# Weight-conversion passes regrouped at the end of a step's VectorE work, in an attention + rational-MLP kernel

## The chip, the cores and the metric

The kernel runs on one core of a Trainium2 chip. The time is device microseconds of that core, the median of repeated runs.

## What is computed

Attention over 4 batches and 8 heads (576 positions, head size 64) with a position bias, then an MLP whose nonlinearity is a quotient of two polynomials:

```python
    scores = scale * np.matmul(q, k.transpose(0, 1, 3, 2))
    scores = scores + bias.transpose(2, 0, 1)[None, :, :, :]
    attn = softmax(scores)
    x = (attn @ v) as (2304, 512)
    h = x @ w_in                                # 512 -> 2048
    P = a[0] + a[1] * h + a[2] * h**2 + a[3] * h**3
    Q = 1.0 + np.abs(b[0]) * np.abs(h) + np.abs(b[1]) * h**2
    out = (P / (Q + 1e-06)) @ w_out             # 2048 -> 512
```

`w_in` and `w_out` come as 64-bit floats and are turned into a high and a low 32-bit part on the chip.

## The kernel before

**Two halves.** Attention fills the first 270 us. The MLP fills the rest. Its 2304 rows are cut into five blocks (384, 512, 512, 512, 384 rows, `TS`, L27), and its 2048 hidden features into 16 groups of 128. Two passes over the five blocks are made, each with half of the features, because the split weights of one half fill the buffers. A block takes four **steps** (`FPR` = 4) of 256 features each, so there are 40 steps, counted from 0: steps 0 to 3 are block 0 of pass one, 4 to 7 block 1, 16 to 19 block 4, and 20 to 39 pass two.

**A step s** (the loop at L853) issues, in this order: the first product `mm1(s)` on TensorE (24 matmuls, `h` in PSUM, from the split rows `xh`, `xl` and the split weights); the second product `mm2(s-2)` (output tiles `o`); for step s-1, three ScalarE operations `rat1` (L725 to L727, the reciprocal of Q by Ln and Exp), three VectorE operations `dv2`, `dv3`, `dv4` (L746, L753, L760: `gh`, the high part of the quotient, and `m`); `evac` (L813: ScalarE copies finished output tiles of a block out of PSUM); for step s, `rat0` (L720, L721: two ScalarE reads of `h`), and `dvu`, `dv0`, `dv1` (L730, L736, L739: three VectorE operations that read `h` from PSUM); for step s-1 `pl1` (L767: GpSimd makes `gl`, the low part of the quotient, from `m`). Then, in even steps, `split_x` (L302, L303) splits half of the rows of the next block, and SyncE loads the rows of the block after it. All queues keep the order in which the program writes (`tc.manual_schedule()`).

**The late weights.** Ten of the 16 feature groups are converted during attention. Those of the last six (`LATE`) are converted inside pass one: 12 **jobs**, one for each group and matrix. A job (`w_conv`, L116) is a load of the same 0.5 MB twice at two offsets (`wx`, `wy`, L126), and five passes over 128x512 words: `mag` (L142, VectorE), `rebias` (L151, ScalarE), and on VectorE `sign` (L154), `join` (L167) and `low` (L174); then two stores of the result to DRAM (L114), which pass two loads again (`w_load`, L231). The buffers of `wx` and `wy` are one pool of three tiles.

Before, the jobs are placed in half steps, one job every three halves (L833 to L850): half 2s comes ahead of `rat0(s)`, half 2s+1 at the end of step s. The first job has its `mag` in half 2, the next in half 5, and so on; `sign`, `join` and `low` follow two halves after `mag`, and right behind them the load of the next job is issued, one half step ahead of that job's own `mag`. So every second job has `sign`, `join`, `low` right behind `dv4`, and `mag` at the end of a step; the others have it the other way round.

**Across blocks.** `mm2` of a new block writes the PSUM tiles of the block before, so it waits for `evac`. `evac` stands behind `rat1(s-1)` in ScalarE's queue, and `rat1(s-1)` waits for `dvu(s-1)` on VectorE. `e_norm(NU - 1)` (L400, one VectorE product and a store) finishes the last attention tile inside step 4; rows of it are read by the load at the end of step 6.

Of the kernel before, what the change touches and what calls it, by code (L numbers as in the profile page):

```python
# [8 lines left out]
F32 = mybir.dt.float32  # L9
# [7 lines left out]
P = 128  # L17
# [18 lines left out]
def tile_attn_moe(  # L36
# [14 lines left out]
    cpool = ctx.enter_context(tc.tile_pool(name="cpool", bufs=1))  # L51
# [31 lines left out]
        for d_, nm in ((woh, "woh"), (wol, "wol")):  # L83
            d_[g] = pool.tile([P, 2, DM], F32R, tag=f"{nm}{g}", name=f"{nm}{g}")

    fill = cpool.tile([P, 112], F32, tag="fill", name="fill")
    nc.gpsimd.memset(fill[:, 0:8], 0.0)
    stg = ctx.enter_context(tc.tile_pool(name="stg", bufs=2))
    bpool = ctx.enter_context(tc.tile_pool(name="bpool", bufs=2))
# [4 lines left out]
    U16 = mybir.dt.uint16  # L94
    FN = KD * P
# [13 lines left out]
    def w_out_to(f, part, hi, lo):  # L109
        d = wsc.get((f, part)) or dpool.tile([P, 2, KD, P], F32, tag=f"ws{f}_{part}", name=f"ws{f}_{part}")  # L110
        wsc[f, part] = d
        for i, t in enumerate((hi, lo)):
            if t is not None:
                nc.sync.dma_start(out=d[:, i], in_=t.bitcast(F32))  # L114

    def w_conv(f, part):  # L116
        st = {}
        here = f < 6
        eng = G if f < KF - LATE else V

        def load():
            w = (w_in, w_out)[part]

            def get(nm, o, src):
                t = stg.tile([P, 4 * FN + 4], U16, tag="wx", name=f"{nm}{f}_{part}", bufs=3)
                nc.sync.dma_start(out=t[:, o:o + 4 * FN], in_=src)  # L126
                return t

            x = get("wx", 0, w.bitcast(U16)[f])[:, 0:4 * FN]
            st["u"] = x.bitcast(U32).rearrange("p (f t) -> p f t", t=2)[:, :, 1]  # L130
            if eng is G:
                st["h"] = x.rearrange("p (f t) -> p f t", t=4)[:, :, 1:3]
            else:
                y = get("wy", 1, w.bitcast(U16)[f])[:, 2:4 * FN + 2]
                st["m"] = y.bitcast(U32).rearrange("p (f t) -> p f t", t=2)[:, :, 0]

        def tl(nm, dt, bufs=1):
            st[nm] = stg.tile([P, FN], dt, tag=nm, name=f"{nm}{f}_{part}", bufs=bufs)
            return st[nm]

        def mag():
            V.tensor_scalar(  # L142
                out=tl("wk", U32), in0=st["u"], scalar1=0x7FFFFE00, scalar2=None, op0=ALU.bitwise_and
            )

        def rows(t):
            return t.rearrange("p (k f) -> p k f", k=KD)

        def rebias():
            st["wh"] = rows(tl("wh", U32, 2))  # L150
            A.activation(out=st["wh"], in_=rows(st["wk"]), func=AF.Relu, bias=wmin, scale=8.0)  # L151

        def sign():
            V.scalar_tensor_tensor(  # L154
                out=st["wh"], in0=rows(st["u"]), scalar=0x80000000, in1=st["wh"],
                op0=ALU.bitwise_and, op1=ALU.bitwise_or,
            )

        def mid():
            if eng is G:  # L160
                st["m"] = tl("wm", U32)
                m = st["m"].bitcast(U16).rearrange("p (f t) -> p f t", t=2)
                G.tensor_copy(out=m, in_=st["h"])

        def join():
            st["x"] = st["m"] if eng is G else tl("wk", U32)
            V.scalar_tensor_tensor(  # L167
                out=rows(st["x"]), in0=rows(st["m"]), scalar=13, in1=st["wh"],
                op0=ALU.logical_shift_right, op1=ALU.bitwise_or,
            )  # L170

        def low():
            st["wl"] = w_hilo(f, part)[1] if here else rows(tl("wl", F32R, 2))
            eng.tensor_tensor(  # L174
                out=st["wl"], in0=rows(st["x"]).bitcast(F32), in1=st["wh"].bitcast(F32), op=ALU.subtract
            )

        def store(hi=True, lo=True):
            if not here:
                w_out_to(f, part, st["wh"] if hi else None, st["wl"] if lo else None)  # L180
            elif hi:
                nc.sync.dma_start(out=w_hilo(f, part)[0].bitcast(F32), in_=st["wh"].bitcast(F32))

        return [load, [mag], [rebias], [sign, join, low, store], mid]
# [18 lines left out]
    def w_job(f, part):  # L203
        return w_conv(f, part) if wide else w_plain(f, part)
# [15 lines left out]
    def w_hilo(f, part):  # L220
        g, j = divmod(f % KH, 2)
        if part == 0:
            return wih[g][:, :, j * P:(j + 1) * P], wil[g][:, :, j * P:(j + 1) * P]
        return (
            woh[g][:, j, :].rearrange("p (k f) -> p k f", k=KD),
            wol[g][:, j, :].rearrange("p (k f) -> p k f", k=KD),
        )
# [5 lines left out]
    with tc.manual_schedule():  # L233
# [3 lines left out]
        with ExitStack() as actx:  # L237
# [334 lines left out]
            with ExitStack() as bctx:  # L572
# [66 lines left out]
                for y, n in enumerate(order):  # L639
# [6 lines left out]
                    pool, nm = (ps_sc, "sc")  # L646
                    if y in (NG - 3, NG - 1):
                        pool, nm = (ps_mx, "mx")
                    elif y % 3 == 1:
                        pool, nm = (ps_tp, "tp")  # L650
                    pa = pool.tile([P, 2, 512], F32, tag=nm, name=f"pb{n}")
                    cuts = sorted({0, mid, 512, EW})
                    for a, z in zip(cuts, cuts[1:]):
                        o = pa[:, a // 512, a % 512:a % 512 + z - a]
                        for c in range(4):
                            x = rows[n, c]
                            x = x[:, a - mid:z - mid] if a >= mid else x[:, mid - a:mid - z:-1]
# [43 lines left out]
        with ExitStack() as mctx:  # L701
# [21 lines left out]
            def rat1(s):  # L723
                u, r0 = rt[s, "u"], et(s, "r0", 2)
                A.activation(out=u, in_=u, func=AF.Abs)  # L725
                A.activation(out=r0, in_=u, func=AF.Ln, bias=qc)  # L726
                A.activation(out=r0, in_=r0, func=AF.Exp, scale=-1.0)  # L727
# [44 lines left out]
            FPR = KH // 2  # L772
# [32 lines left out]
            part, pre = {}, {}  # L805
# [15 lines left out]
            def load_part(t):  # L821
                for c in range(TS[t] // P):
                    o = ep.tile([P, DM], F32, tag="o", name=f"pre{t}_{c}", bufs=4)
                    nc.sync.dma_start(out=o, in_=part.pop((t, c)))
                    pre[t, c] = o

            jobs = [
                w_job(f + j, y) for f in range(KF - LATE, KF, 2) for y in range(2) for j in range(2)
            ]
            J0 = 2  # L830
            jobs[0][0]()

            def job(h):  # L833
                for c, j in enumerate(jobs):
                    d = h - J0 - 3 * c
                    if d == 2:
                        for x in j[3]:
                            x()
                        if c + 1 < len(jobs):
                            jobs[c + 1][0]()  # L840
                    if d == 0:
                        for x in j[1]:
                            x()

            def job_act(s):
                for h in (2 * s - 1, 2 * s):
                    c, d = divmod(h - J0, 3)
                    if 0 <= c < len(jobs) and d == 0:
                        for x in jobs[c][2]:
                            x()  # L850

            LAG = 2
            for s in range(NQ + LAG + 1):  # L853
                def at(d):
                    return 0 <= s - d < NQ

                n, fp = divmod(s, FPR)
                if s < NQ:
                    if n >= NTT and fp == 3:
                        load_part(n % NTT)  # L860
                    for x in ([s] if 1 < s < NQ - 2 else [s, s + 1] if s == NQ - 2 else []):
                        mm1(x, 0)
                        mm1(x, 1)
                late = list(evq)
                evq.clear()
                if n > NTT:
                    evac(late)
                    late = []
                if at(LAG):
                    mm2(s - LAG)  # L870
                if at(1):
                    rat1(s - 1)
                    dv2(s - 1)
                    dv3(s - 1)
                    dv4(s - 1)
                evac(late)
                if at(0):
                    job(2 * s)
                    rat0(s)
                    job_act(s)  # L880
                    dvu(s)
                    dv0(s)
                    dv1(s)
                if at(1):
                    pl1(s - 1)
                for y in range(2):
                    fl = s - NTT * FPR + FPR - 3 * y
                    if 0 <= fl < FPR:
                        for j in range(2):
                            w_load(KH + 2 * fl + j, y)  # L890
                if s == FPR:
                    e_norm(NU - 1)
                if at(0):
                    job(2 * s + 1)
                if at(0) and n + 1 < NR:
                    for k in ((0, 1), (), (2, 3), ())[fp]:
                        [x() for x in split_x(n + 1, k)]
                    if fp == 2 and n + 2 < NR:
                        load_x(n + 2, (n + 2) % NTT)
# [78 lines left out]
```

## Time and profile before

| what | value |
|---|---|
| median of 3 runs | 691.81 us (690.77 to 691.98) |
| profiled execution, its own time | 689.72 us |
| span of the profiled execution | 687.9 us, mean granted TensorE clock 0.989 |
| PE (matmul) busy | 664.3 us, 97% |
| PEld (weight load) busy | 551.5 us, 80% |
| DVE busy | 573.9 us, 83% |
| ACT busy | 471.4 us, 69% |
| POOL busy | 156.6 us, 23% |

PE is TensorE, DVE VectorE, ACT ScalarE, POOL GpSimd, SP SyncE (its queue issues the DMAs). Busy shares are averages over the two halves and the two passes, which have different limits; the rows further down are of pass one of the MLP, where the change is. An idle time is put down to the instruction that released the engine last.

### The profile page before, as it was taken

The page shows a single profiled execution, that of the slowest core. Times are in us where ns is not written, and L with a number is a line of the kernel's source. Part 1 is how long each engine was busy: PE and PEld are TensorE (multiplying, and loading weights), DVE is VectorE, ACT ScalarE, POOL GpSimd, SP SyncE. Part 2 cuts the span into 40 slices and gives each one's busy share as a digit, 9 for nine tenths or more (in the row PEclk, how much of TensorE's full clock was granted, in tenths as well). Part 3 has the DMA queues.
Part 4 walks back from the last instruction along what each step waited for, and adds up shares of the span by engine and source line. Part 5 has one row for each costly group of instructions (what it writes and reads, how often), then busy time and mean ns, then how long its engine had stood idle before and what let it go on. Part 6 is the DMA issues. An engine that isn't in the chain of part 4 may idle for free.

```text
span 687.9 us, 16078 instructions
## 1 busy us (share of the span) xinstructions
PE 664.3 (97%) x6274; PEld 551.5 (80%) x6274; DVE 573.9 (83%) x1012; ACT 471.4 (69%) x721; POOL 156.6 (23%) x108
## 2 busy tenths in 40 slices
PE   9999999999999999986899999969999999999997
PEld 6667888888888888974788887868988888888996
DVE  7986888888888994979988999889777878778766
ACT  8978899988888986554756466456656555465461
POOL 0000233433333320211122112212222212122211
PEclk9999999999999999999899999998999999999999
DMA  6886887789689682262532543449560401303031
GB/s 238 301 319 214 291 281 262 248 247 295 218 282 286 212 270 84 82 192 81 190 127 79 180 136 132 162 149 344 199 202 0 152 17 62 108 0 123 0 108 46
DMA packets 74843, 118.96 MB, mean 173 GB/s; under 512 B 11905, under 2 KB 33809, under 8 KB 74769
## 3 DMA queue, kind: packets, MB, share of 16 engines
q1 hardware_dynamic: 74624, 117.79, 51.7%
q8 instruction: 49, 0.80, 0.5%
q14 instruction: 26, 0.20, 0.1%
q10 hardware_dynamic: 144, 0.16, 0.1%
HBM read 79.17 MB, written 35.61 MB: 167 GB/s over the span
## 4 chain that ended last, share of the span: by engine, by line
PE 71%; DVE 13%; ACT 6%; DMA 5%; issue 4%; SPq 0%; DVEq 0%; ACTq 0%
PE o L797 18%; PE h L318 16%; PE mx L451 13%; PE sc L342 12%; PE tp L411 5%; PE pb L658 5%; DMA wx<-in_w_out_dram 3%; DVE wk L167 3%; DVE m L753 2%; DVE gh L746 2%; DVE u L730 2%; ACT r L726 2%; ACT u L725 2%; DMA wx<-in_w_in_dram 1%; DVE wh L154 1%
## 5 line engine op out<-in xcount | busy, mean ns | idle before, releaser
L767 POOL TENSOR_TENSOR gl<-m,r 128x1024 fp32r<-128x1024 f32 (+1 forms) x39 | 87.3, 2238 | 324.3 <-DVE m L760 284.7
L352 DVE CUSTOM_DVE_ANT_0 s<-sc,bias 128x576 f32<-128x576 f32 x144 | 103.2, 753 | 11.6 <-PE sc L342 6.6
L368 ACT ACTIVATE p<-s,m 128x576 f32<-128x576 f32 x144 | 110.7, 772 | 1.6 <-DVE m L352 1.6
L797 PE MATMUL o<-woh,gh 128*128 128x512 f32 x216 | 86.8, 402 | 15.1 <-ACT os L813 15.1
L720 ACT ACTIVATE w<-h,babs 128x1024 f32<-128x1024 f32 (+1 forms) x40 | 41.2, 1031 | 81.3 <-PE h L318 81.3
L451 PE MATMUL mx<-pt,v 128*64 128x128 f32 (+1 forms) x1600 | 95.1, 267 | 0.0
L342 PE MATMUL sc<-k,q 64*128 64x288 f32 (+1 forms) x640 | 91.2, 426 | 0.5 <-DVE m L352 0.4
L419 ACT COPY pt<-tp 128x1024 f32<-128x1024 f32 x72 | 72.6, 1008 | 24.5 <-PE tp L411 24.2
L797 PE MATMUL o<-wol,gh 128*128 128x512 f32 x216 | 86.2, 399 | 0.0
L725 ACT ACTIVATE u<-u 128x1024 f32<-128x1024 f32 (+1 forms) x40 | 39.0, 976 | 67.5 <-DVE u L730 67.1
L451 PEld LDWEIGHTS mx<-pt,v 128*64 128x64 f32 x1600 | 78.5, 137 | 5.0 <-issue 0.2
L730 DVE SCALAR_TENSOR_TENSOR u<-w,babs,h 128x1024 f32<-128x1024 f32 (+1 forms) x40 | 46.8, 1170 | 29.6 <-ACT t L721 29.4
L318 PE MATMUL h<-xb,wih 128*128 128x512 f32 (+1 forms) x240 | 69.2, 369 | 1.9 <-DVE xb L303 1.3
L342 PEld LDWEIGHTS sc<-k,q 64*128 64x128 f32 (+1 forms) x640 | 49.4, 175 | 20.4 <-DVE m L352 7.1
L797 PEld LDWEIGHTS o<-woh,gh 128*128 128x128 f32 x216 | 41.9, 194 | 24.9 <-ACT os L813 16.2
L746 DVE SCALAR_TENSOR_TENSOR gh<-t,cst,r 128x1024 fp32r<-128x1024 f32 (+1 forms) x40 | 46.9, 1173 | 13.7 <-ACT r L727 11.3
L797 PE MATMUL o<-woh,gl 128*128 128x512 f32 x216 | 53.8, 389 | 0.0
L318 PEld LDWEIGHTS h<-xb,wih 128*128 128x128 f32 x240 | 44.4, 188 | 9.0 <-DVE xb L303 1.8
L753 DVE SCALAR_TENSOR_TENSOR m<-u,qc,gh 128x1024 f32<-128x1024 f32 (+1 forms) x40 | 47.1, 1178 | 4.0
L411 PE MATMUL tp<-ident,p 64*128 64x64 f32 x1152 | 49.3, 223 | 0.0
L797 PEld LDWEIGHTS o<-wol,gh 128*128 128x128 f32 x216 | 41.9, 194 | 8.6
L760 DVE SCALAR_TENSOR_TENSOR m<-t,cst,m 128x1024 f32<-128x1024 f32 (+1 forms) x40 | 47.1, 1178 | 1.4
(81 smaller groups left out, 1324.2 us busy)
## 6 DMA issues: line engine op xcount, KB each, us to landing
tab<-e SPq DMA_DIRECT2D x36, 295.5 KB, 4.1
wx<-in_w_in_dram SPq DMA_DIRECT2D x16, 512.0 KB, 6.0
wx<-in_w_out_dram SPq DMA_DIRECT2D x16, 512.0 KB, 4.6
v<-in_vp_dram SPq DMA_DIRECT2D x16, 320.0 KB
ws<-wh SPq DMA_DIRECT2D x20, 256.0 KB
ws<-wl SPq DMA_DIRECT2D x20, 256.0 KB, 3.2
q<-in_qt_dram SPq DMA_DIRECT2D x16, 288.0 KB
k<-in_kt_dram SPq DMA_DIRECT2D x16, 288.0 KB, 6.0
```

The lines of the kernel that those rows point to most:

```text
L318: T.matmul(hps[s][:, j, :w_], w[:, k, sl], x[:, k, :w_], start=(k == 0 and z == 0), stop=(k == KD - 1 and z == 2),)
L342: T.matmul(sc[i, j][o, a, :SH], q[r, x], k[r, a * SH:(a + 1) * SH], start=True, stop=True,)
L352: V.tensor_tensor_reduce(out=t.rearrange("p (a s) -> p a s", a=2), in0=sc.pop((i, j))[:, :, :SH], in1=bias[p][:, 5 * j + c, :].rearrange(" ...
L368: A.activation(out=prob[i][:, z * S:z * S + S], in_=t, func=AF.Exp, bias=m, scale=-1.0, accum_out=sums[u % 4][:, k:k + 1],)
L411: T.transpose(out, pb[x, k0:k0 + P], ident[x, x])
L419: A.copy(out=t[:, 0:8].rearrange("p x (r s) -> p r x s", r=2), in_=ps)
L451: T.matmul(ps[y, o], vt[n][:, kc, y], t[:, 2 * kc + j if kc < 4 else 8, o], start=(kc == 0), stop=(kc == 4),)
L730: V.scalar_tensor_tensor(out=et(s, "u", 2), in0=rt[s, "w"], scalar=babs[:, 0:1], in1=hp(s), op0=ALU.add, op1=ALU.mult,)
L746: V.scalar_tensor_tensor(out=hi, in0=rt[s, "t"], scalar=abs_[:, 0:1], in1=rt[s, "r0"], op0=ALU.add, op1=ALU.mult,)
L753: V.scalar_tensor_tensor(out=m, in0=rt[s, "u"], scalar=qc, in1=rt[s, "gh"].bitcast(F32), op0=ALU.add, op1=ALU.mult,)
L767: eng.tensor_tensor(out=lo, in0=rt[s, "m"], in1=rt[s, "r0"], op=ALU.mult)
L797: T.matmul(po[n, c], l[:, j, c * P:(c + 1) * P], r[fp][:, j, :], start=(first and x is a), stop=(last and x is z),)
```

## The change

The jobs have one place now, the end of a step's VectorE work. Two jobs start in every three steps: `mag` of jobs 0, 1, 2, ... stands at the end of steps 2, 3, 5, 6, 8, 9, ... 17, 18. `rebias` stands behind `rat0` of the step after, and `sign`, `join`, `low` and the stores at the end of that step, ahead of the next `mag` where there is one. Right behind the `mag` of a job the load of the next one is issued, which has a fourth buffer in the `wx` pool (all loads of that pool rotate over four, those during attention too). `e_norm(NU - 1)` moves from step 4 to step 5, the sixth. `fill`, of which 8 columns are used, grows from 112 to 232 columns, which moves the tiles allocated behind it. No arithmetic is added or taken away.

```diff
-    fill = cpool.tile([P, 112], F32, tag="fill", name="fill")
+    fill = cpool.tile([P, 232], F32, tag="fill", name="fill")
...
-                t = stg.tile([P, 4 * FN + 4], U16, tag="wx", name=f"{nm}{f}_{part}", bufs=3)
+                t = stg.tile([P, 4 * FN + 4], U16, tag="wx", name=f"{nm}{f}_{part}", bufs=4)
...
-            def job(h):
-                for c, j in enumerate(jobs):
-                    d = h - J0 - 3 * c
-                    if d == 2:
-                        for x in j[3]:
-                            x()
-                        if c + 1 < len(jobs):
-                            jobs[c + 1][0]()
-                    if d == 0:
-                        for x in j[1]:
-                            x()
-
-            def job_act(s):
-                for h in (2 * s - 1, 2 * s):
-                    c, d = divmod(h - J0, 3)
-                    if 0 <= c < len(jobs) and d == 0:
-                        for x in jobs[c][2]:
-                            x()
+            at_ = {3 * (c // 2) + c % 2 + J0: c for c in range(len(jobs))}
+
+            def job(s, stage):
+                c = at_.get(s - (stage > 1))
+                if c is not None:
+                    for x in jobs[c][stage]:
+                        x()
+                    if stage == 1 and c + 1 < len(jobs):
+                        jobs[c + 1][0]()
...
                 if at(0):
-                    job(2 * s)
                     rat0(s)
-                    job_act(s)
+                    job(s, 2)
...
-                if s == FPR:
+                if s == FPR + 1:
                     e_norm(NU - 1)
                 if at(0):
-                    job(2 * s + 1)
+                    job(s, 3)
+                    job(s, 1)
```

VectorE's queue in step 2, before: the first job's `sign`, `join`, `low` (lines L154, L167, L174) stand right behind the three operations of step 1 that release GpSimd, and ahead of those of step 2; the second job's `mag` (L142) stands at the step's end, ahead of the split of rows (L303).

```order
-L746 SCALAR_TENSOR_TENSOR gh_5413<-t_5352,cst,r_5409 128x2x384
-L753 SCALAR_TENSOR_TENSOR m_5415<-u_5357,qc,gh_5413 128x2x384
-L760 SCALAR_TENSOR_TENSOR m_5415<-t_5352,cst,m_5415 128x2x384
-L154 SCALAR_TENSOR_TENSOR wh_0_5355<-wx_0_5324,wh_0_5355 128x512
-L167 SCALAR_TENSOR_TENSOR wk_0_5419<-wy_0_5326,wh_0_5355 128x512
-L174 TENSOR_TENSOR wl_0_5421<-wk_0_5419,wh_0_5355 128x512
-L730 SCALAR_TENSOR_TENSOR u_5434<-w_5430,babs,h_5363 128x2x384
-L736 TENSOR_TENSOR t_5431<-t_5431,h_5363 128x2x384
-L739 SCALAR_TENSOR_TENSOR t_5431<-t_5431,cst,h_5363 128x2x384
-L142 TENSOR_SCALAR wk_0_5440<-wx_0_5426 128x512
```

VectorE's queue in step 3 of the change, where the first job's passes stand now:

```order
+L746 SCALAR_TENSOR_TENSOR gh_5484<-t_5415,cst,r_5480 128x2x384
+L753 SCALAR_TENSOR_TENSOR m_5486<-u_5418,qc,gh_5484 128x2x384
+L760 SCALAR_TENSOR_TENSOR m_5486<-t_5415,cst,m_5486 128x2x384
+L730 SCALAR_TENSOR_TENSOR u_5495<-w_5489,babs,h_5437 128x2x384
+L736 TENSOR_TENSOR t_5490<-t_5490,h_5437 128x2x384
+L739 SCALAR_TENSOR_TENSOR t_5490<-t_5490,cst,h_5437 128x2x384
+L154 SCALAR_TENSOR_TENSOR wh_0_5493<-wx_0_5324,wh_0_5493 128x512
+L167 SCALAR_TENSOR_TENSOR wk_0_5502<-wy_0_5326,wh_0_5493 128x512
+L174 TENSOR_TENSOR wl_0_5504<-wk_0_5502,wh_0_5493 128x512
+L142 TENSOR_SCALAR wk_0_5509<-wx_0_5426 128x512
```

Three operations that read `h` from PSUM (L730, L736, L739) now stand between the release of GpSimd's product and the job's passes, and the `mag` of the next job follows them in the same step.

SyncE's queue around the first loads, before (`xr` are the rows of a later block, `ws` the stores of converted weights):

```order
L114 DMA ws_0_5423<-wh_0_5355 128x512
L114 DMA ws_0_5423<-wl_0_5421 128x512
L126 DMA wx_0_5426<-in_w_in_dram 128x2048
L126 DMA wy_0_5428<-in_w_in_dram 128x2048
L289 DMA xr_5446<-xd_72 128x4x256
L289 DMA xr_5446<-xd_73 128x4x256
L114 DMA ws_0_5518<-wh_0_5505 128x512
L114 DMA ws_0_5518<-wl_0_5516 128x512
L126 DMA wx_1_5521<-in_w_out_dram 128x2048
L126 DMA wy_1_5523<-in_w_out_dram 128x2048
```

and of the change:

```order
L126 DMA wx_0_5426<-in_w_in_dram 128x2048
L126 DMA wy_0_5428<-in_w_in_dram 128x2048
L289 DMA xr_5434<-xd_72 128x4x256
L289 DMA xr_5434<-xd_73 128x4x256
L114 DMA ws_0_5506<-wh_0_5493 128x512
L114 DMA ws_0_5506<-wl_0_5504 128x512
L126 DMA wx_1_5511<-in_w_out_dram 128x2048
L126 DMA wy_1_5513<-in_w_out_dram 128x2048
L114 DMA ws_0_5584<-wh_0_5571 128x512
L114 DMA ws_0_5584<-wl_0_5582 128x512
```

The load of job 1 (`wx_0_5426`) stood behind the stores of job 0 and now stands ahead of them; that of job 2 (`wx_1_`) stood behind the stores of job 1 and now stands behind those of job 0.

## Rows read from the trace of the kernel before

**Rows 1.** Windows: 268 to 475 us, busy us by engine, granted clock, DMA

```profile
268.00:475.00 207.00, 190.04 (x875) 160.19 (x872) 182.05 (x186) 120.53 (x144) 41.74 (x18) 0.97 0.45 148
```

**Rows 2.** Waits, 268 to 464 us: total us, times, longest us

```profile
ACT u L725 <- DVE u L730: 46.1, 12, 7.5
...
PE o L797 <- ACT os L813: 15.1, 3, 9.2
```

**Rows 3.** PE's timeline: start, us; in brackets idle before, releaser

```profile
293.35 0.70 PE L318 MATMUL h<-xb,wih 128*128 128x512 f32 x2 [0.57 <-DVE t L739]
...
296.53 0.50 PE L318 MATMUL h<-xb,wih 128*128 128x512 f32 x1 [1.32 <-DVE xb L303]
...
329.09 0.80 PE L797 MATMUL o<-woh,gh 128*128 128x512 f32 x1 [9.15 <-ACT os L813]
...
463.84 0.80 PE L797 MATMUL o<-woh,gh 128*128 128x512 f32 x1 [5.28 <-ACT os L813]
```

**Rows 4.** The chain that ended last: start us, us, what

```profile
329.09 7.09 PE o L797 x24
...
373.02 6.46 DMA wx<-in_w_out_dram
...
463.84 6.54 PE o L797 x18
...
474.56 4.12 PE o L797 x18
...
536.39 5.44 PE o L797 x24
```

**Rows 5.** DVE groups, 268 to 475 us; last row whole kernel

```profile
L167 DVE SCALAR_TENSOR_TENSOR wk<-wy,wh 128x512 uint32<-128x512 uint32 x12 | 19.6, 1636 | 0.4
...
L142 DVE TENSOR_SCALAR wk<-wx 128x512 uint32<-128x512 uint32 x12 | 6.6, 553 | 13.7 <-DMA wx<-in_w_out_dram 9.4 <-DMA wx<-in_w_in_dram 4.4
...
L142 DVE TENSOR_SCALAR wk<-wx 128x512 uint32<-128x512 uint32 x32 | 18.8, 587 | 13.7 <-DMA wx<-in_w_out_dram 9.4 <-DMA wx<-in_w_in_dram 4.4
```

**Rows 6.** Timelines of POOL (gl) and DVE (join, L167)

```profile
320.05 2.63 POOL L767 TENSOR_TENSOR gl<-m,r 128x1024 fp32r<-128x1024 f32 x1 [9.87 <-PE h L318]
...
320.51 2.71 DVE L167 SCALAR_TENSOR_TENSOR wk<-wy,wh 128x512 uint32<-128x512 uint32 x1
...
332.86 2.42 POOL L767 TENSOR_TENSOR gl<-m,r 128x1024 fp32r<-128x1024 f32 x1 [10.19 <-ACT wh L151]
...
336.96 0.69 DVE L167 SCALAR_TENSOR_TENSOR wk<-wy,wh 128x512 uint32<-128x512 uint32 x1
```

**Rows 7.** DVE's timeline, at 384 rows (128x768) and 512

```profile
283.66 1.02 DVE L746 SCALAR_TENSOR_TENSOR gh<-t,cst,r 128x768 fp32r<-128x768 f32 x1 [0.85 <-ACT r L727]
...
286.70 0.68 DVE L154 SCALAR_TENSOR_TENSOR wh<-wx,wh 128x512 uint32<-128x512 uint32 x1
...
300.10 1.00 DVE L730 SCALAR_TENSOR_TENSOR u<-w,babs,h 128x768 f32<-128x768 f32 x1
...
302.93 0.68 DVE L154 SCALAR_TENSOR_TENSOR wh<-wx,wh 128x512 uint32<-128x512 uint32 x1
...
304.99 1.01 DVE L746 SCALAR_TENSOR_TENSOR gh<-t,cst,r 128x768 fp32r<-128x768 f32 x1
...
310.39 1.27 DVE L730 SCALAR_TENSOR_TENSOR u<-w,babs,h 128x1024 f32<-128x1024 f32 x1
...
314.02 0.75 DVE L400 TENSOR_TENSOR xs<-xs,rb 128x576 f32<-128x576 f32 x1
...
315.89 1.28 DVE L746 SCALAR_TENSOR_TENSOR gh<-t,cst,r 128x1024 fp32r<-128x1024 f32 x1
```

**Rows 8.** ACT's timeline at 512 rows, and block 0's copies

```profile
312.16 1.06 ACT L725 ACTIVATE u<-u 128x1024 f32<-128x1024 f32 x1
...
315.46 1.10 ACT L720 ACTIVATE w<-h,babs 128x1024 f32<-128x1024 f32 x1
...
328.47 1.54 ACT L813 COPY os<-o 128x512 f32<-128x512 f32 x3
```

## The prediction

> **What bounds the kernel now.** I read the page's busy shares first, then the chain that ended last, then PE's timeline, then DVE's. The shares say PE (97%), but the chain runs without a break through PE only before 270 us and after 464 us; between the two, pass one of the MLP, it passes again and again through DVE, ACT and weight loads. The windows show that stretch apart: in 207 us PE is busy 190.0, at a mean clock of 0.97, and DVE 182.1 [rows 1]. PE's waits there are few and long. Matmuls of h wait 0.57 and 1.32 us, and those of o wait three times for a copy of output tiles, 15.1 us in all, 9.15 at 329.09 and 5.28 at 463.84 [rows 2, 3]. That copy is late because ACT stands at L725 for DVE's L730, 46.1 us in total [rows 2]: DVE is behind, and a block's last step shows it. The clock's loss lies behind the two long ones: the first group of matmuls after each is slow, 24 in 7.09 us where 24 take 5.44 at 2.4 GHz, and 18 in 6.54 where 18 take 4.12 [rows 4]; they ran in part at 1.2 GHz, after an idle PE.
>
> So the prize is known. PE loses 0.57 + 1.32 + 15.1 = 17.0 us in waits, and (7.09 - 5.44) + (6.54 - 4.12) = 4.1 us at the lower clock: **21.1 us** in pass one. Steps 20 to 39 run PE end to end, so nothing is to be had there.
>
> **Why DVE is behind.** Two rows say it. `mag` waits for its load: 13.7 us over 12 passes, and this is all that `mag` waits in the whole kernel [rows 5]. And `join` takes 1636 ns in the mean, 19.6 us for 12 [rows 5]: six take 0.69 us, like that at 336.96, and six take 2.2 to 2.8, like that at 320.51 [rows 6]. The slow ones stand right behind `dv4`, whose end releases gl on POOL: gl runs from 320.05 to 322.68 and the join that began at 320.51 ends at 323.22; the gl of 332.86 was over by 335.28, before the fast one began [rows 6]. The excess is 19.6 - 12 x 0.69 = 11.3 us. Waits and excess make 25 us of DVE's queue, about what PE loses.
>
> **What the change removes.** *Joins.* Each now has `dvu`, `dv0`, `dv1` between `dv4` and itself, 2.83 us at 384 rows and 3.63 at 512 [rows 7], where gl takes 2.42 undisturbed [rows 6]. gl begins 0.2 us after `dv4` (315.89 + 3.9 = 319.8; 3.9 is 320.51 - 315.89 less 0.7 for `sign` [rows 6, 7]). I take 0.69 for all 12: 11.3 us off DVE. The Trainium skill, SBUF — State Buffer, section Who interferes with whom, says that a VectorE instruction with two SBUF inputs and a GpSimd instruction that reads SBUF exclude each other, and that whichever starts first blocks the other for its whole length. The pair of rows agrees; it would extend to `mag`, `low` and the splits, and is a rival's price below.
>
> *Load waits.* A load is now issued about a step before its `mag` (10.88 us of PE at 512 rows, 8.24 at 384: two groups of 5.44 or 4.12 [rows 4]). The longest in the chain took 6.46 us [rows 4]. I take zero, with 4.5 us of cover at 512 rows and 1.8 at 384; bounds zero and 13.7.
>
> *Steps 2 to 5, where DVE is tightest.* PE would be ready for the first `mm2` of block 1 at 293.35 - 0.57 = 292.78 [rows 3], plus `mm1(4)` 5.44, `mm2(2)` 4.12, `mm1(5)` 5.44, `mm2(3)` 4.12, `mm1(6)` 5.44: 317.3. DVE, from the `dv2` of step 1 (283.66, less 0.4 for the `mag` that is no longer in that step), without idle time:
> - step 2: dv2 to dv4 3.04, the three reads of h 2.83, `mag` 0.5, split 1.2: 7.6
> - step 3: 3.04 + 2.83 + sign, join, low 2.06 + 0.5: 8.4
> - step 4: 3.04 + 3.63 + 2.06 + 1.2: 9.9
> - step 5, to the end of `dvu`: 3.9 + 1.2: 5.1
>
> which ends at 314.3 [rows 5, 7] (split: 315.89 - 314.02 less 0.7 for the normalisation). ACT then needs 3.30 for `rat1` and 0.62 for the first copy [rows 8]: 318.2. PE waits **0.9 us** in place of 9.15, and the 0.57 and 1.32 go too, since the split of step 2 ends near 290.9, ahead of 292.78. The 1.32 us wait cost no clock, so I charge none to 0.9. Moving the normalisation out of step 4 takes its 0.7 off this path; in step 5 it stands behind `dvu`, and step 6 reads its store.
>
> *Steps 6 to 19.* Four steps of 512 rows now ask DVE for 4 x (3.9 + 3.63) + two splits 2.4 + 8/3 jobs at 2.56 = 39.4 us, and PE for 43.5: DVE falls back under PE, 4.1 us in each block. At 384 rows it is 4 x 5.87 + 2.4 + 6.8 = 32.7 against 33.0, just covered. For the wait at 463.84: from the end of `mm1(17)` PE has 5.44 + 4.12 = 9.6 us of other work, and the way to the copy takes, at durations for 512 rows, 2 x 1.10 (`rat0`) + 1.2 + 3.30 + 0.62 = 7.3 [rows 7, 8]. It goes, and its clock loss with it. Next late after that would be the loads of pass two, behind jobs in SP's queue; they stand no later relative to PE than before.
>
> *At nothing:* the fourth buffer during attention (no `mag` waits there, so an earlier load meets no one; bounds 1 us either way, the spread of the three runs), the shifted addresses (same bounds), `rebias` (same place on ACT, no longer behind a late `mag`).
>
> **Sum.** 21.1 - 0.9 = 20.2 us. The profiled execution took 689.72 us (span 687.9): 669.5 by it. The runs shown have a median 2.1 us higher, and I take the gain off that: 691.81 - 20.2 = **671.6 us**.
>
> **Rivals.**
> - *DVE stays behind in steps 2 to 5.* Should the `mag` of steps 2 and 3 wait for their loads by 3 us each (more than twice the mean of rows 5, 13.7 over 12), 318.2 becomes 324.2, PE waits 6.9 and pays the clock again (1.65): 20.2 - 6 - 1.65 = 12.5, so 679.3. For it: at this point DVE has no slack at all. Against: both loads are issued a step early and into free buffers.
> - *gl comes later than I think, and meets the job at the step's end.* At 2.07 more for 12 joins DVE gets 24.8 us; three blocks cover 4.1 each, 12.5 show: 684. By the skill's rule `mag` and splits in the steps without a join would be held as well, so 18 steps in place of 12, 37 us, of which 25 show: 696. Against both: 1.2 us of room at 512 rows and 0.8 at 384 if gl keeps its 0.2 us start, with its 384-row form shorter still.
> - *Loads held in SP's queue (slower).* The load of a job now stands behind the stores of the job before it, and in some steps behind output copies, all in order. Place: the `mag` at a step's end. If copies come as late as they did (9.15 [rows 3]) and the load takes 6.46, it lands 15.6 us after its turn, 4.7 after its `mag`'s. Twelve such waits are 56 us; less 12.3 of cover, 44 show: 715. It decides from 2.7 us a job on (12 x 2.7 - 12.3 = 20). Against: copies were late because DVE was, and DVE is not.
> - *Nothing happens,* as PE at 97% suggests: then ACT or PE itself would be the limit in pass one. Against: in this stretch DVE is busy for 182.1 of 207 us, 88%, weight loads for 160.2, 77% [rows 1], and the waits lead to DVE. PE's waits would have to be refilled by another engine: 691.8. The Trainium skill, Perfetto Trace Analysis, section Identifying the Most-Contended Engine, says that matmul busy time does not tell how close TensorE is to its limit, and to take weight-load busy time instead; by that DVE, not PE, is the engine to relieve here, as the waits have it.
>
> **Chances.** Forecast 0.73, with 669 to 674 as its own range; behind in steps 2 to 5 0.14; gl 0.06; loads 0.04; nothing 0.03. Low: all 21.1 us and 2 us for the attention edits and the spread of runs, 668.5. High: the first rival's 679.3 rounded up to 680; beyond lie 0.13. Within 0.2% (1.4 us, what a measurement tells from no change): 0.04; slower 0.04; faster 0.92.
>
> **What would show it.** In the profile after: `join` near 0.69 us in the mean of 12; `mag` with no wait for DMA; the waits of o for the copy near 1 us in all; the clock at 1.00 through pass one; after 320 us a chain of PE alone, mm1 and mm2 in turn. I am wrong if joins are fast and `mag` does not wait and PE still stands, or if joins or `mag` stay slow at the step's end.

## The result, and the profile after

The changed kernel takes **668.79 us** (median of 5 runs, 668.36 to 669.28), against 690.77 of the kernel before in the same comparison (5 runs, 688.51 to 691.98): 0.9685 of it, 95% interval 0.9663 to 0.9707. The two profiled executions took 689.72 and 668.79 us, their spans are 687.9 and 667.0 us: 20.9 us by either. The forecast was 671.6 us, 20.2 us less.

| what | before | after |
|---|---|---|
| span | 687.9 | 667.0 |
| PE busy | 664.3, 97% | 659.4, 99% |
| PEld busy | 551.5 | 548.4 |
| DVE busy | 573.9 | 559.5 |
| ACT busy | 471.4 | 471.5 |
| mean granted TensorE clock | 0.989 | 0.999 |

The page's part on the chain that ended last, by engine, in the kernel after:

```profile
PE 95%; DVE 2%; ACT 1%; issue 1%; DVEq 0%; POOL 0%; ACTq 0%; POOLq 0%
```

Before, PE had 71% of that chain, DVE 13% and DMA 5%. The stretch from 268 to 475 us of the kernel after, as in [rows 1] (busy us by engine, granted clock, DMA):

```profile
268.00:475.00 207.00, 205.90 (x975) 176.69 (x974) 186.59 (x204) 133.69 (x158) 45.59 (x21) 1.00 0.52 174
```

PE is busy for 205.9 us of the 207, where it was for 190.0, and the granted clock reads 1.00, where it read 0.97. The waits [rows 2], 262 to 454 us:

```profile
ACT u L725 <- DVE u L730: 20.6, 14, 4.4
...
PE o L797 <- ACT os L813: 1.1, 1, 1.1
```

The three waits for output copies, 15.1 us in all, have become one of 1.1. ACT still waits for DVE's L730, but 20.6 us and not 46.1. Only the longest of these waits, 4.4 us in step 5, still reaches PE, as its 1.1 us. DVE's groups [rows 5], 262 to 475 us:

```profile
L167 DVE SCALAR_TENSOR_TENSOR wk<-wy,wh 128x512 uint32<-128x512 uint32 x12 | 8.3, 692 | 0.4
...
L142 DVE TENSOR_SCALAR wk<-wx 128x512 uint32<-128x512 uint32 x12 | 5.1, 424 | 0.2
```

All 12 joins take 0.69 us, and the 12 `mag` no longer wait for a load (13.7 us before; the 0.2 here has no releaser). That is 11.3 + 13.7 us taken out of DVE's queue. The chain in order of time [rows 4]; what stands between these lines is PE alone, mm1 and mm2 in turn:

```profile
318.13 5.75 PE o L797 x24
...
323.88 5.44 PE h L318 x24
...
329.32 5.44 PE o L797 x24
...
445.32 4.12 PE o L797 x18
```

Here is how the tight steps 2 to 5 went, on POOL, DVE and ACT [rows 6 to 8]:

```profile
302.35 1.85 POOL L767 TENSOR_TENSOR gl<-m,r 128x768 fp32r<-128x768 f32 x1 [6.60 <-DVE m L760]
...
302.10 1.27 DVE L730 SCALAR_TENSOR_TENSOR u<-w,babs,h 128x1024 f32<-128x1024 f32 x1
...
305.74 0.69 DVE L154 SCALAR_TENSOR_TENSOR wh<-wx,wh 128x512 uint32<-128x512 uint32 x1
...
306.45 0.69 DVE L167 SCALAR_TENSOR_TENSOR wk<-wy,wh 128x512 uint32<-128x512 uint32 x1
...
312.90 1.27 DVE L730 SCALAR_TENSOR_TENSOR u<-w,babs,h 128x1024 f32<-128x1024 f32 x1
...
317.51 1.54 ACT L813 COPY os<-o 128x512 f32<-128x512 f32 x3
```

In step 4 gl runs from 302.35 to 304.20, while DVE reads h from PSUM (from 302.10, the trio is over at 305.7); the join begins at 306.45, 2.2 us after gl, and is not held. `dvu` of step 5 ends at 314.17, the first copy begins at 317.51, and PE starts on block 1 at 318.13, 11.0 us earlier than before (329.09).

### The profile page after: what moved, and what is told of

It is laid out like the page before. It is cut to its first block, busy times and chain, and to the rows that moved or that the text cites. A ratio compares the mean times of both kernels' runs of the same rounds, so it can differ in the third digit from the quotient of the medians.

```text
span 667.0 us, 16086 instructions
## 1 busy us (share of the span) xinstructions
PE 659.4 (99%) x6274; PEld 548.4 (82%) x6274; DVE 559.5 (84%) x1012; ACT 471.5 (71%) x721; POOL 154.9 (23%) x108
## 4 chain that ended last, share of the span: by engine, by line
PE 95%; DVE 2%; ACT 1%; issue 1%; DVEq 0%; POOL 0%; ACTq 0%; POOLq 0%
PE o L797 29%; PE h L318 28%; PE mx L451 13%; PE sc L342 13%; PE pb L658 6%; PE tp L411 5%; PE mx L411 1%; PE warm L598 1%; DVE ring L619 1%; DVE u L730 0%; ACT r L726 0%; ACT u L725 0%; DVE m L753 0%; DVE xl L303 0%; DVE gh L746 0%
## 5 line engine op out<-in xcount | busy, mean ns | idle before, releaser
L767 POOL TENSOR_TENSOR gl<-m,r 128x1024 fp32r<-128x1024 f32 (+1 forms) x39 | 85.5, 2193 | 304.1 <-DVE m L760 260.5
L797 PE MATMUL o<-woh,gh 128*128 128x512 f32 x216 | 84.3, 390 | 1.1 <-ACT os L813 1.1
L797 PE MATMUL o<-wol,gh 128*128 128x512 f32 x216 | 84.2, 390 | 0.0
L730 DVE SCALAR_TENSOR_TENSOR u<-w,babs,h 128x1024 f32<-128x1024 f32 (+1 forms) x40 | 46.9, 1172 | 37.2 <-ACT t L721 37.1
L342 PEld LDWEIGHTS sc<-k,q 64*128 64x128 f32 (+1 forms) x640 | 49.1, 175 | 20.2 <-DVE m L352 6.7
L797 PEld LDWEIGHTS o<-woh,gh 128*128 128x128 f32 x216 | 40.5, 188 | 9.8 <-ACT os L813 1.5
L739 DVE SCALAR_TENSOR_TENSOR t<-t,cst,h 128x1024 f32<-128x1024 f32 (+1 forms) x40 | 47.0, 1175 | 1.4
```

Source lines behind the costliest of these rows:

```text
L342: T.matmul(sc[i, j][o, a, :SH], q[r, x], k[r, a * SH:(a + 1) * SH], start=True, stop=True,)
L739: V.scalar_tensor_tensor(out=rt[s, "t"], in0=rt[s, "t"], scalar=abs_[:, 1:2], in1=hp(s), op0=ALU.add, op1=ALU.mult,)
L767: eng.tensor_tensor(out=lo, in0=rt[s, "m"], in1=rt[s, "r0"], op=ALU.mult)
L797: T.matmul(po[n, c], l[:, j, c * P:(c + 1) * P], r[fp][:, j, :], start=(first and x is a), stop=(last and x is z),)
```

## The experiments

Each is compared with the kernel before on the same chip. Its median was 689.91 us beside the fourth buffer alone, the loads a job ahead, the twelve joins beside gl and the three buffers, and 690.11 us beside the others. The theory: late loads and joins beside gl both made DVE late, and DVE's lateness at a block's end is what PE paid for. Rivals: only the loads; only the joins; the buffer, the addresses or the normalisation.

### The fourth buffer alone

```diff
--- before
-    fill = cpool.tile([P, 112], F32, tag="fill", name="fill")
+    fill = cpool.tile([P, 232], F32, tag="fill", name="fill")
...
-                t = stg.tile([P, 4 * FN + 4], U16, tag="wx", name=f"{nm}{f}_{part}", bufs=3)
+                t = stg.tile([P, 4 * FN + 4], U16, tag="wx", name=f"{nm}{f}_{part}", bufs=4)
```

> The kernel before, with the fourth buffer and the wider fill alone. Theory (they cost and gain nothing by themselves): 690 to 692 us, the attention half unchanged, mag's wait in the MLP still 12 to 14 us. Rival (the earlier loads or the shifted addresses act in attention): a difference of over 1.4 us either way, in the first 270 us.

690.50 us (688.78 to 692.14, 12 runs), ratio 1.0013 (1.0001 to 1.0024). DVE's `mag` group, 262 to 490 us:

```profile
L142 DVE TENSOR_SCALAR wk<-wx 128x512 uint32<-128x512 uint32 x12 | 7.0, 586 | 14.8 <-DMA wx<-in_w_out_dram 9.4 <-DMA wx<-in_w_in_dram 5.4
```

and from the table of waits PE's for the copies, in the same stretch:

```profile
PE o L797 <- ACT os L813: 15.2, 3, 9.1
```

The same lateness, the same waits; the interval allows at most 0.24%, and that on the slower side. In the attention half, 45 to 262 us, PE is busy for 215.81 us in both kernels. Buffer and addresses gain nothing by themselves; they were priced at nothing.

### Loads a job ahead, places as before

```diff
--- before, with four buffers and the wider fill
                         for x in j[3]:
                             x()
-                        if c + 1 < len(jobs):
-                            jobs[c + 1][0]()
                     if d == 0:
                         for x in j[1]:
                             x()
+                        if c + 1 < len(jobs):
+                            jobs[c + 1][0]()
```

> The places of before, with the fourth buffer and each load issued behind the mag of the job before it. Theory (late loads and joins beside gl each made VectorE late): mag's wait for loads falls from 13.7 us to under 1, six joins stay at 2.2 to 2.8 us (19.6 us for 12), PE's waits for the output copy fall from 15.1 us to 4 to 9, and the time lands near 680 us, between the two kernels. Rival (the loads were all of it): 669 to 671 us. Rival (the joins were all of it): 687 us or more.

677.78 us (676.34 to 678.09), ratio 0.9818 (0.9802 to 0.9834). Two DVE groups, 262 to 490 us:

```profile
L167 DVE SCALAR_TENSOR_TENSOR wk<-wy,wh 128x512 uint32<-128x512 uint32 x12 | 19.7, 1640 | 0.4
...
L142 DVE TENSOR_SCALAR wk<-wx 128x512 uint32<-128x512 uint32 x12 | 5.0, 420 | 0.0
```

PE's timeline at its one wait for a copy:

```profile
324.24 0.80 PE L797 MATMUL o<-woh,gh 128*128 128x512 f32 x1 [6.77 <-ACT os L813]
```

and the piece of the chain behind that wait:

```profile
324.24 8.65 PE o L797 x24
```

The load waits are gone and six joins are as slow as before. The rest of PE's waits for copies went, but the one at the end of block 0 stayed at 6.8 us, and its 24 matmuls took 8.65 us in place of 5.44. So the loads alone give a little over half of the gain, 0.9818 against 0.9685, and neither rival holds: with early loads DVE has room enough in the blocks of 512 rows to absorb slow joins, not in steps 2 to 5.

### Joins in their new place, loads late

```diff
--- after, with three buffers and the narrow fill
-                    if stage == 1 and c + 1 < len(jobs):
+                    if stage == 3 and c + 1 < len(jobs):
                         jobs[c + 1][0]()
```

> The changed kernel, but the load of the next job is issued behind the stores of this one, as before, with three buffers. Theory: joins stay at 0.69 us; the second job of each pair has its mag right behind the issue of its load and waits 4 to 6 us, 25 to 35 us in all on VectorE; with 12 us of room 13 to 23 show, 682 to 692 us. Rival (late loads alone are hidden): 669 to 672 us.

688.27 us (687.66 to 689.69, 10 runs), ratio 0.9973 (0.9963 to 0.9983). DVE's groups, 262 to 490 us:

```profile
L167 DVE SCALAR_TENSOR_TENSOR wk<-wy,wh 128x512 uint32<-128x512 uint32 x12 | 8.3, 693 | 0.4
...
L142 DVE TENSOR_SCALAR wk<-wx 128x512 uint32<-128x512 uint32 x12 | 5.1, 424 | 29.2 <-DMA wx<-in_w_in_dram 15.1 <-DMA wx<-in_w_out_dram 14.1
```

and PE's waits there:

```profile
PE o L797 <- ACT os L813: 10.2, 3, 4.6
...
PE o L797 <- POOL gl L767: 3.3, 2, 1.8
```

The joins are fast, and the kernel is still nearly as slow as before: six `mag` of twelve wait 4.9 us in the mean, 29.2 us. The time is 19.5 us above the changed kernel (688.27 - 668.79), but the three buffers have a part in that: against the kernel with three buffers and early loads (670.80, further down) it is 17.5. Against the kernel before, the new place takes 11.3 us of slow joins out of DVE's queue and puts 15.5 us of load waits in (29.2 - 13.7). Being in the right place is worth little when the load is issued one instruction ahead of its use.

### All twelve joins beside gl, loads early

```diff
--- after
                 if at(0):
+                    job(s, 2)
+                    job(s, 3)
                     rat0(s)
-                    job(s, 2)
                     dvu(s)
...
                 if at(0):
-                    job(s, 3)
                     job(s, 1)
```

> The changed kernel, with sign, join and low of all 12 jobs put back right behind dv4 (rebias ahead of rat0, so that they need not wait for it); loads stay a job ahead. Theory: all 12 joins take 2.2 to 2.8 us, about 24 us more VectorE time; with 4.1 us of room in each of three blocks about 12 us show: 680 to 683 us. Rival (the join's place matters only through the first block, the rest has room enough): 670 to 674 us. If joins stay at 0.69 us, their place beside gl is not what made them slow.

683.25 us (683.07 to 683.38), ratio 0.9905 (0.9891 to 0.9918): 14.5 us above the changed kernel, at the upper edge of the theory's range. The join group, 262 to 490 us:

```profile
L167 DVE SCALAR_TENSOR_TENSOR wk<-wy,wh 128x512 uint32<-128x512 uint32 x12 | 31.0, 2586 | 0.4
```

PE's timeline at its three waits for copies:

```profile
321.54 0.80 PE L797 MATMUL o<-woh,gh 128*128 128x512 f32 x1 [4.37 <-ACT os L813]
...
369.41 0.50 PE L797 MATMUL o<-woh,gh 128*128 128x512 f32 x1 [1.63 <-ACT os L813]
...
416.68 0.80 PE L797 MATMUL o<-woh,gh 128*128 128x512 f32 x1 [3.45 <-ACT os L813]
```

and the chain behind the last:

```profile
416.68 8.38 PE o L797 x24
```

Every join takes 2.2 to 2.8 us, 22.7 us more in all (31.0 - 8.3). PE waits at the end of three blocks, 9.5 us, and pays the clock behind two of the waits. The place makes the join slow, with the same data, the same shape and no load to wait for. `rebias` on ACT moved with the joins; what that costs by itself was not measured.

### What gl holds

```diff
--- after
                     dv4(s - 1)
+                    probe(s)
...
+            def probe(s):
+                o, t, m = fill[:, 8:232], rt[s - 1, "t"][:, 0, :224], rt[s - 1, "m"][:, 0, :224]
+                for i in range(3):
+                    if s % 3 == 0:
+                        V.tensor_tensor(out=o, in0=t, in1=m, op=ALU.mult)
+                    elif s % 3 == 1:
+                        V.tensor_scalar(out=o, in0=t, scalar1=2.0, scalar2=None, op0=ALU.mult)
```

> The changed kernel with three short VectorE operations of 224 columns, whose result nobody reads, right behind dv4: in every third step tensor_tensor with both inputs in SBUF, in the step after it tensor_scalar with one input in SBUF, in the third none. Undisturbed they should take 0.3 to 0.4 us. Theory (gl on GpSimd holds what VectorE shares with it): one of the three ends only when gl ends, 2 us late, for both kinds. Rival (only the integer join is hit): none is late.

One execution; its 707.34 us (probes in 27 steps) measures nothing else. The two groups of probes, by the tile they write (count, then ns min/median/max):

```profile
L849 DVE TENSOR_SCALAR fill<-t x42: 268/277/2479, 279.1 to 696.3; 128x224 f32<-128x224 f32 x42
...
L847 DVE TENSOR_TENSOR fill<-t,m x39: 391/393/2476, 295.9 to 688.4; 128x224 f32<-128x224 f32 x39
```

and the timelines of DVE (a whole triple, its second probe, and the last triple) and of POOL (the gl beside the first):

```profile
295.94 2.77 DVE L847 TENSOR_TENSOR fill<-t,m 128x224 f32<-128x224 f32 x3
...
296.37 1.91 DVE L847 TENSOR_TENSOR fill<-t,m 128x224 f32<-128x224 f32 x1
...
695.67 0.89 DVE L849 TENSOR_SCALAR fill<-t 128x224 f32<-128x224 f32 x3
...
296.08 1.95 POOL L767 TENSOR_TENSOR gl<-m,r 128x768 fp32r<-128x768 f32 x1 [5.66 <-DVE m L760]
```

Undisturbed, a probe takes 0.39 us with two SBUF inputs and 0.27 with one; the longest of each kind takes 2.48. In the triple shown the first began at 295.94, ahead of gl (296.08), and ran through; the second, from 296.37, was held until gl was over (298.03) and took 1.91 us; the triple ended at 298.71. All 26 triples beside a gl go this way, and in the last, at 695.67, where GpSimd has no gl to run, all three probes together take 0.89 us. `dvu`, which reads h from PSUM and one SBUF tile, never lost time beside gl: 1.27 to 1.28 us at 512 rows, with or without. So it is not only the integer join that suffers; operations of these two kinds do when they start while gl runs. The kernel before shows it for `mag` too: the one that began at 446.72, after a wait for its load, took 1.85 us beside a gl that ran from 445.89 to 448.29, where most take 0.42 or 0.43. The Trainium skill, SBUF — State Buffer, section Who interferes with whom, states both kinds (two SBUF inputs, against a GpSimd instruction that reads SBUF, as gl does; a `tensor_scalar` in its two-port mode), and that an instruction with at most one SBUF input outside that mode is free. Its rule agrees with these rows; that the probe with one input ran in that mode is not shown by a row of its own.

### Three buffers

```diff
--- after
-    fill = cpool.tile([P, 232], F32, tag="fill", name="fill")
+    fill = cpool.tile([P, 112], F32, tag="fill", name="fill")
...
-                t = stg.tile([P, 4 * FN + 4], U16, tag="wx", name=f"{nm}{f}_{part}", bufs=4)
+                t = stg.tile([P, 4 * FN + 4], U16, tag="wx", name=f"{nm}{f}_{part}", bufs=3)
```

> The changed kernel with three wx buffers and the old width of fill. Theory (place and time of issue do it, the buffer little): mag needs only the first of a job's two loads, and that finds a free buffer; mag's wait under 2 us in all, time within 0.3% of the changed kernel, 668 to 671 us. Rival (the fourth buffer is what brings the loads in time): mag waits several us in each pair of jobs, 674 us or more.

670.80 us (670.68 to 673.11), ratio 0.9732 (0.9715 to 0.9750); the profiled execution was the one of 673.11. The `mag` group, 262 to 490 us:

```profile
L142 DVE TENSOR_SCALAR wk<-wx 128x512 uint32<-128x512 uint32 x12 | 5.1, 425 | 0.2
```

The timelines of SP's queue, ACT and PE:

```profile
272.82 0.43 SPq L126 DMA_DIRECT2D wx<-in_w_in_dram  x1
...
296.67 0.33 SPq L126 DMA_DIRECT2D wy<-in_w_in_dram  x1
...
297.10 1.24 SPq L289 DMA_DIRECT2D xr<-xd  x2
...
306.17 1.14 ACT L302 CAST xh<-xr 128x512 fp32r<-128x512 f32 x2 [5.83 <-DMA xr<-xd]
...
319.78 0.80 PE L797 MATMUL o<-woh,gh 128*128 128x512 f32 x1 [3.26 <-ACT os L813]
```

and the chain behind PE's wait:

```profile
319.78 8.39 PE o L797 x24
```

The time is at the theory's edge and `mag` does not wait, but the reason for the 2 us was in neither expectation. The second load of job 1 needs the buffer that job 0's `sign` frees at 296.67, so SP's queue stands from 273.3 to 296.67. Behind it stands the load of block 2's rows, which goes out at 297.10 where it went at 290.64 in the changed kernel; ACT's cast of those rows waits 5.83 us for it, `rat1` of step 4 stands behind the cast, and PE waits 3.26 us at the end of block 0, 2.2 more than in the changed kernel, and pays the clock. The other three executions, 670.68 to 670.87 us, have no trace; that they waited alike and paid less for the clock would fit, and is not shown. By this trace the fourth buffer is there for the queue, not for `mag`.

### The normalisation back in step 4

```diff
--- after
-                if s == FPR + 1:
+                if s == FPR:
                     e_norm(NU - 1)
```

> The changed kernel with the last normalisation back in step 4. Theory: it lies on VectorE's path to the first output copy, PE's wait there goes from 1.1 to 1.8 us, the time by 0.7 us, under what can be told. Rival (its store or the load of rows behind it held something): a change of over 1.4 us.

668.99 us (668.91 to 669.61), ratio 0.9696 (0.9683 to 0.9710). PE's wait at the end of block 0:

```profile
318.95 0.50 PE L797 MATMUL o<-woh,gh 128*128 128x512 f32 x1 [1.76 <-ACT os L813]
```

1.76 us against 1.1: the 0.7 us of the operation, as expected, and too little to tell in the time.

### Jobs from step 4 on

```diff
--- after
-            J0 = 2
+            J0 = 4
```

> The changed kernel with the first job's mag in step 4 and not in step 2, all jobs two steps later. Theory: VectorE has no job passes ahead of the first output copy, PE's 1.1 us wait goes, 667.5 to 668.5 us. Rival (VectorE gets late at the end, where blocks of 384 rows have no room, or the loads of pass two wait for the last stores): PE waits near steps 18 to 24, 669 us or more.

667.09 us (666.80 to 667.66), ratio 0.9668 (0.9655 to 0.9681); the span is 665.9 against 667.0. PE's chain across the end of block 0:

```profile
311.85 5.44 PE h L318 x24
317.29 5.44 PE o L797 x24
322.73 5.44 PE h L318 x24
```

PE goes from `mm1(6)` into the first `mm2` of block 1 without a wait: in the table of waits none of PE's is left from 300 us on, so the late rival did not come. The time is a little below what the theory expected. All its executions are faster than all of the changed kernel (668.36 at least), in the spans of the profiled ones by 1.1 us, as long as the wait that is gone; the two did not run side by side, and the intervals of their ratios overlap.

## Why the prediction was right

**The prize.** 21.1 us of PE waits and lost clock were read from pass one, and all but a small rest came: from the free PE at 292.78 to the end of the first `mm2` of block 4 (463.84 + 6.54 = 470.38) it was 177.6 us before; after, the same stretch runs from 292.56 to 449.44, 156.9 us. The difference, 20.7, is nearly all of the gain of 20.9.

**Joins.** Forecast 0.69 for all 12, measured 0.692 in the mean; gl was over 2.2 us ahead of the join in the step shown, and 0.88 us where it came closest (the join at 432.27). That the place was the cause was shown by putting all 12 back (683.25 us). One sentence on the kernel before was wrong, without harm to the sum: every second job had both its `mag` and its `sign`, `join`, `low` right behind `dv4` (the first job at 279.55 and 286.70), and the others had both at a step's end (the second at 295.45 and 302.93).

**Load waits.** Forecast zero, measured 0.2 without a releaser. What they were worth by themselves was not forecast; the loads alone show a little over half (677.78 us).

**Steps 2 to 5.** `dvu` of step 5 was to end at 314.3 and ended at 314.17; the first copy to let PE go at 318.2, which it did at 318.13. PE's wait was to be 0.9 and was 1.1, because PE was ready 0.3 us earlier than summed (317.0). "The 1.32 us wait cost no clock, so I charge none" held for the clock, which was granted in full around the 1.1 us wait too:

```profile
316.00:324.00 8.00, 6.90 (x31) 5.39 (x30) 7.82 (x9) 7.83 (x11) 2.20 (x1) 1.00 0.74 203
```

Yet the 24 matmuls behind that wait took 5.75 us, not 5.44. So 0.3 us were lost beside the wait without any loss of clock, and the sum had nothing for that.

**Steps 6 to 19.** "DVE falls back under PE" held: the table of waits has none of PE's after the 1.1 us, in the blocks of 384 rows either.

**The sum.** 20.2 against 20.9 by profiled executions. The term that was too small is the list of PE's losses, 21.1 us: 177.6 us less the work in that stretch (24 groups at 5.44, 3 at 4.18 and 3 at 4.12, 155.5) is 22.1. No wait was overlooked. In the stretch of the kernel before PE is busy for 160.65 us, and the 16.95 left over are the five waits of the list:

```profile
292.78:470.38 177.60, 160.65 (x703) 133.31 (x704) 157.49 (x156) 104.52 (x123) 37.69 (x16) 0.96 0.45 151
```

What the list lacked is busy time: 160.65 - 155.5 is 5.1 us, and it had 4.1, the two groups at the lower clock. Most of the 1.0 us between them lies in groups beside the shorter waits, as with the 5.75 us above.

The forecast of 671.6 us was 2.8 us too high: 668.79 lies just under its own range of 669 to 674 and 0.3 us above the low end of 668.5. Only 0.7 of the 2.8 is the gain. The other 2.1 came from taking a gain that was read in the profiled execution (689.72) off the median of 691.81; off 689.72 it gives 669.5. Between the medians of the comparison the gain is 22.0 us (690.77 - 668.79), more than the profiles show. The executions of the kernel before differ in clock: of the 17 beside the first experiments, the 6 with a mean granted clock of 0.989, as in the profile, have a median of 688.9 us and the 11 with 0.987 one of 690.1. So the profile that was read had lost less to the clock than most.

**The rivals.** All four were kept out by what had been held against them, and two of their prices could be tried. Joins beside gl: 684 forecast, 683.25 measured when they were put there; the working (24.8 us, less 12.3 of room) was right in the first term (22.7) and lucky in the sum: the room was there, but PE also paid the clock, which the sum left out, and a start of 671.6 that was 2.8 us too high hid part of it. Late loads: the formula (what DVE waits, less 12.3 of room) gives 29.2 - 12.3 = 16.9 us for the kernel with late loads, which showed 17.5 against the kernel with three buffers and early loads. The mechanism of loads held in SP's queue exists, with three buffers, and costs 2 us there, through the rows of a later block and not through `mag`.

**Normalisation, buffer, addresses.** Priced at nothing or at 0.7 us on a path; measured 0.7 us of wait (1.76 against 1.1) and no time that can be told.

## What to carry to other kernels

When the busiest engine stands at a block's end, follow the wait back to the engine whose queue is late, and list what in that queue is not work: waits for loads, and operations that take three times their own length. Place VectorE operations with two SBUF inputs, or a `tensor_scalar` out of SBUF, where GpSimd is idle, and put operations that read PSUM and one SBUF tile beside GpSimd's work; issue a load a full step ahead of its first use, with enough buffers that the queue of loads does not stand behind a buffer that is still read. Background work costs least where the engine has room: starting it after the tight steps took away PE's last wait, about a microsecond.

## What was not expected of the hardware

In these rows the clock's price does not follow the length of the wait. Behind a PE wait of 9.15 us, 24 matmuls took 7.09 us [rows 4]; behind 6.77 us they took 8.65, behind 3.45 us 8.38, and behind 3.26 us 8.39, all against 5.44 at full clock. Behind waits of 1.1 and 1.76 us they took 5.75 and 5.74 at a granted clock of 1.00, so by these two about 0.3 us of each of the others is not the clock's either. Windows of the kernel before (PE busy is the second number, the granted clock the one ahead of the last two):

```profile
322.00:325.00 3.00, 0.00 (x0) 0.00 (x0) 2.96 (x3) 0.00 (x0) 0.68 (x1) 1.00 0.07 27
325.00:328.00 3.00, 0.00 (x0) 0.00 (x0) 2.56 (x3) 2.70 (x3) 0.00 (x0) 0.52 0.97 285
328.00:331.00 3.00, 1.91 (x5) 1.53 (x6) 2.53 (x3) 3.00 (x6) 0.00 (x0) 0.50 0.69 274
331.00:334.00 3.00, 3.00 (x13) 2.41 (x12) 2.96 (x4) 2.85 (x6) 1.14 (x1) 0.84 0.30 115
```

PE ended its last matmul near 320, the clock was at 1.2 GHz (0.50) from about 325, and PE began again at 329.09: some of the slow time passed while it stood. Windows of the kernel with three buffers:

```profile
317.00:319.00 2.00, 0.00 (x0) 0.00 (x0) 2.00 (x3) 1.95 (x2) 0.20 (x1) 0.90 0.00 0
319.00:321.00 2.00, 1.22 (x3) 1.04 (x4) 1.89 (x3) 2.00 (x5) 0.00 (x0) 0.50 0.66 199
321.00:323.00 2.00, 2.00 (x7) 1.54 (x6) 1.96 (x2) 2.00 (x3) 0.00 (x0) 0.50 0.54 211
323.00:325.00 2.00, 2.00 (x6) 1.60 (x5) 2.00 (x3) 1.94 (x4) 1.55 (x1) 0.50 0.00 0
325.00:327.00 2.00, 2.00 (x9) 1.60 (x8) 1.97 (x3) 1.88 (x3) 0.85 (x1) 0.89 0.00 0
```

PE stood from 316.5 to 319.78, the clock fell about a microsecond before PE began again, and stayed at 1.2 GHz for some 6 us of work. So a shorter wait need not cost less through the clock: with the loads alone PE waited 2.4 us less at the end of block 0 than before and lost 1.6 us more behind it.
